# Asking for the small first load, lam, on ScalarE's queue instead of SyncE's

## The chip, the cores and the metric

The kernel runs on one core of a Trainium2 chip. The metric is the device time of one execution in microseconds (us); lower is better. The time quoted for a kernel is the median of its timed runs. A profile is one execution recorded by the hardware profiler; its span runs from the first to the last instruction of the core.

## The reference

The computation is a decayed linear attention over blocks, followed by a gated causal convolution and two projections, all in float32 at 4 batches, 8 heads, 768 positions and 64 channels to a head (the three `moe_` matrices are float64 on the host):

```python
Dmask   = where(i >= j, lam[h] ** (i - j), 0)            # per head, in a block of 64
lam_pow = lam[h] ** (i + 1);  rev_pow = lam[h] ** (63 - i)
for each block of 64 positions:
    intra = ((q k^T) * Dmask) v
    inter = (q * lam_pow) kv_state
    out   = intra + inter
    kv_state = lam[h] ** 64 * kv_state + (k * rev_pow)^T v
x    = out with the heads side by side                   # 4 x 768 x 512
gate = sigmoid(causal convolution of x, 5 taps, per channel, conv_w)
result = (gate * (x @ w_val)) @ w_out
```

`lam` holds eight numbers, one decay to a head. Everything else is built from them and from the four large inputs.

## The kernel before

The kernel works in 12 steps, each of 128 positions of two batches. For each step it loads two tiles of 1 MiB: `lq` (q and k, transposed, line 354, piece `ld.i.0` of the order) and `lv` (v and k by token, line 354, piece `ld.i.2`). The weights come in four loads of 1 MiB, `w_raw` (line 373): two for `w_val` (`wv.0`, `wv.1`) and two for `w_out` (`wo.0`, `wo.1`). A load of 20 KB brings `conv_w` (line 454). Results go out in pieces of 128 or 256 KB.

The order of all work after the opening is written out by hand in the string `ORDER`: each engine runs its instructions in that order, and the framework adds the semaphores. All transfers are requested by SyncE (`SP`) in the order of the string, so a request that has to wait holds up those behind it. The string begins

```
ld.0.0:lq0 dm.0 dm.1 qe ld.0.2:lv0 kd.0.0 s.0.0:s0,s1 kd.0.1 m.0.0.0:A0 s.0.1:u1,u2 m.0.1.0 ia.0.0:xp0 wv.0:g0
ld.1.0:lq1 ld.1.2:lv1 wv.1:g1 m.0.0.1:A1 m.0.1.1 ia.0.1 f.0:u3 wv.0.0.e:val0 ld.2.0:lq2 ...
```

Ahead of the string stands an opening that is not in it. Its first transfer is `lam`, repeated on the host for the 128 partitions (128 x 8 floats, 4 KB, line 191). Then come the identity (GpSimd, `masks.py`), a tile of zeros (VectorE, line 196), a first sigmoid on ScalarE that brings its table load to the front (line 199), and nine warming matmuls on TensorE (line 205; the trace counts them as 18).

Two pieces read `lam`. `dm.0` and `dm.1` (line 233) make the decay mask `mask_c` by eight scans on VectorE, one to a head. `qe` (lines 243 and 246) makes the powers `qdec_c` by repeated doubling on GpSimd. The first reader of the mask is `m.0.0.0` (line 565), which multiplies the first scores (`s.0.0`, TensorE, line 542, from `lq`) by it; it stands behind all eight scans on VectorE. The result `A` goes with `lv` into `ia.0.0` (line 607). The widening of the weights (`wv.0.0.e` and the pieces after it, lines 278 to 320) begins on VectorE when the first `w_raw` has landed; TensorE first needs its product in `v.0.0` (line 946).

On ScalarE nothing of the string comes before the widening of the first weight (line 290).

Of the kernel before, what the change touches and what calls it, by code (L numbers as in the profile page):

```python
# [140 lines left out]
def decay_attention_then_gated_conv(  # L141
# [9 lines left out]
    nc = tc.nc  # L151
# [36 lines left out]


    lam_bc = const.tile([P, H], F32, name="lam_bc")  # L190
    nc.sync.dma_start(lam_bc, lam)
    sdec = const.tile([P, H, D], F32, name="sdec")
    ident = sdec.rearrange("p h d -> p (h d)")[:, :P]
    make_identity(nc, ident)
# [1022 lines left out]
```

## Time and profile before

| | |
|---|---|
| median of 3 runs | 203.88 us |
| runs | 203.19 to 203.99 us |
| profiled execution | 203.55 us |
| its span | 201.6 us |
| mean granted TensorE clock | 1.000 |
| TensorE matmul, busy share of the span | 96% |
| VectorE, busy share | 90% |
| ScalarE, busy share | 65% |
| GpSimd, busy share | 70% |
| `lam` load, request to landing | 1.6 us |

The profile names engines PE (TensorE matmul), PEld (TensorE weight load), DVE (VectorE), ACT (ScalarE), POOL (GpSimd) and SP (SyncE); a `q` behind a name means the engine's sequencer, which issues transfers and waits. `out<-in` are the program's tiles. Times within a trace are microseconds from the start of the span.

### The profile page before, as it was taken

What the parts mean: (1) busy time and instruction counts of PE and PEld (TensorE: products, weight loads), DVE (VectorE), ACT (ScalarE), POOL (GpSimd) and SP (SyncE); (2) the same over time, 40 slices, a digit from 0 to 9 for tenths busy, and PEclk for the clock granted to TensorE, in tenths of its full rate; (3) what the DMA queues carried; (4) which work ended last, traced back from release to release, by engine and by line L of the source; (5) the groups of instructions that cost most, each with busy time, mean ns of one, the idle gap of its engine ahead of it and who ended that gap; (6) DMA issues with size and microseconds to landing.
All of it is one profiled execution on the core that took longest, in us unless ns stands there. A gap on an engine that the chain in (4) does not pass through costs nothing.

```text
span 201.6 us, 7521 instructions
## 1 busy us (share of the span) xinstructions
PE 193.8 (96%) x3282; PEld 166.6 (83%) x3282; DVE 180.9 (90%) x285; ACT 132.1 (65%) x262; POOL 141.8 (70%) x128
## 2 busy tenths in 40 slices
PE   7689999999999999999999999999999999999993
PEld 7568999999899997899888878788777878788882
DVE  5778999998869988998997999999999989999990
ACT  2069589697975698757266455997379953457812
POOL 5447457897799299928946999999959997653000
PEclk9999999999999999999999999999999999999999
DMA  5999999990609103970595992000002210000245
GB/s 180 419 431 423 418 429 419 424 395 26 215 18 367 42 3 83 345 307 3 197 306 187 333 351 99 3 3 7 0 3 104 107 49 3 0 0 2 104 163 202
DMA packets 7952, 36.15 MB, mean 179 GB/s; under 512 B 1136, under 2 KB 1392, under 8 KB 4336
## 3 DMA queue, kind: packets, MB, share of 16 engines
q1 hardware_dynamic: 7920, 35.68, 46.1%
q8 instruction: 25, 0.41, 0.8%
q14 instruction: 7, 0.06, 0.1%
HBM read 29.38 MB, written 6.29 MB: 177 GB/s over the span
## 4 chain that ended last, share of the span: by engine, by line
PE 73%; DVE 9%; DMA 9%; ACT 4%; SPq 2%; issue 1%; ACTq 0%; DVEq 0%
PE vp L946 20%; PE op L1151 18%; PE seven_X L888 11%; DMA lq<-in_qkv 9%; PE xp L592 4%; PE xp L629 4%; PE s L552 4%; PE st L654 4%; PE seven_yz L888 3%; DVE acc L793 3%; PE seven_Z L888 1%; ACT s_part L840 1%; DVE w_sum L405 1%; DVE w_sum L412 1%; SPq L354 1%
## 5 line engine op out<-in xcount | busy, mean ns | idle before, releaser
L793 DVE SCALAR_TENSOR_TENSOR acc<-x,conv_sb,acc 128x512 f32<-128x512 f32 x96 | 70.2, 750 | 5.0 <-ACT acc L791 3.6
L946 PE MATMUL vp<-x_hi,wv_hi 128*128 128x256 f32 (+1 forms) x112 | 34.8, 311 | 0.0
L946 PE MATMUL vp<-x_hi,wv_lo 128*128 128x256 f32 (+1 forms) x112 | 33.5, 299 | 0.3 <-POOL wv_lo L320 0.3
L946 PE MATMUL vp<-x_lo,wv_hi 128*128 128x256 f32 (+1 forms) x112 | 33.4, 298 | 0.0
L1151 PE MATMUL op<-wo_hi,hs 128*128 128x512 f32 x96 | 30.5, 399 | 0.0
L1033 POOL TENSOR_TENSOR hs<-g,hs 128x512 fp32r<-128x512 f32 x12 | 15.9, 1333 | 13.9 <-ACT hs L1022 9.0
L761 POOL TENSOR_TENSOR x_lo<-x,x_hi 128x512 fp32r<-128x512 f32 x18 | 22.9, 1290 | 2.2 <-ACT x_hi L750 2.2
L506 POOL TENSOR_TENSOR qd<-lq,qdec_c 128x512 f32<-128x512 f32 (+1 forms) x18 | 23.1, 1297 | 0.0
L946 PEld LDWEIGHTS vp<-x_hi,wv_hi 128*128 128x128 f32 x112 | 21.3, 190 | 1.6
L946 PEld LDWEIGHTS vp<-x_hi,wv_lo 128*128 128x128 f32 x112 | 21.4, 191 | 1.2 <-POOL wv_lo L320 0.5
L946 PEld LDWEIGHTS vp<-x_lo,wv_hi 128*128 128x128 f32 x112 | 21.4, 191 | 0.6
L791 ACT ACTIVATE acc<-x,conv_sb 128x512 f32<-128x512 f32 x24 | 16.8, 698 | 7.7 <-DVE state L663 7.5
L666 POOL TENSOR_TENSOR sdec<-state,qdec_c 128x512 f32<-128x512 f32 x17 | 20.5, 1207 | 1.0 <-DVE state L663 0.9
L1151 PEld LDWEIGHTS op<-wo_hi,hs 128*128 128x128 f32 x96 | 17.6, 188 | 4.0
L1151 PE MATMUL op<-wo_lo,hs 128*128 128x512 f32 x48 | 18.9, 393 | 0.0
L798 ACT ACTIVATE g<-acc 128x512 f32<-128x512 f32 x24 | 14.0, 597 | 5.7 <-DVE acc L793 5.6
L716 ACT COPY x<-xp 128x512 f32<-128x512 f32 x24 | 12.9, 593 | 3.7 <-PE xp L592 3.2
L1158 ACT COPY o<-op 128x512 f32<-128x512 f32 x16 | 9.4, 587 | 8.0 <-PE op L1151 6.3
L663 DVE TENSOR_TENSOR state<-st,sdec 128x512 f32<-128x512 f32 x17 | 11.7, 686 | 2.0 <-POOL x L723 0.7
L290 ACT ACTIVATE w_em<-w_em,rebias 128x512 int32<-128x512 int32 (+1 forms) x9 | 6.0, 683 | 11.3 <-DVE w_em L278 11.3
L487 ACT ACTIVATE lv<-lv,dmask 128x128 f32<-128x128 f32 x40 | 12.3, 394 | 0.6 <-DMA lv<-in_qkv 0.6
L592 PE MATMUL xp<-A,lv 64*64 64x64 f32 x576 | 12.3, 221 | 0.0
(197 smaller groups left out, 493.4 us busy)
## 6 DMA issues: line engine op xcount, KB each, us to landing
lq<-in_qkv SPq DMA_DIRECT2D x12, 1024.0 KB, 8.0
lv<-in_qkv SPq DMA_DIRECT2D x12, 1024.0 KB, 7.6
out<-o SPq DMA_DIRECT2D x17, 256.0 KB, 3.1
w_raw<-in_w_val SPq DMA_DIRECT2D x2, 1024.0 KB, 12.4
w_raw<-in_w_out SPq DMA_DIRECT2D x2, 1024.0 KB, 17.3
out<-kept SPq DMA_DIRECT2D x6, 256.0 KB, 2.5
out<-o SPq DMA_DIRECT2D x2, 128.0 KB, 2.2
conv_raw<-in_conv_w SPq DMA_DIRECT2D x1, 20.0 KB, 15.8
```

What stands on the lines that cost most here:

```text
L506: nc.gpsimd.tensor_tensor(out=s["qd"][:, hs, ms], in0=lds[i]["qT"][:, u].rearrange("p h (m i) -> p h m i", m=2)[:, :, ms], in1=qdec[:, hs, ...
L592: nc.tensor.matmul(s["xp"][rows(hh), b ^ m, b, g, :], lds[i]["v"][rows(m), b, h * D : (h + 1) * D], s["A"][rows(m), b, h, :], start=b == 0 ...
L666: nc.gpsimd.tensor_tensor(out=sdec, in0=state, in1=qdec_c[:, :, n - 1 : n].to_broadcast([P, H, D]), op=ALU.mult)
L716: nc.scalar.copy(*blocks(s["x"], b))
L761: nc.gpsimd.tensor_tensor(out=s["x_lo"][:, ts], in0=s["x"][:, ts], in1=s["x_hi"][:, ts].bitcast(F32), op=ALU.subtract)
L791: nc.scalar.mul(to, src, w)
L793: nc.vector.scalar_tensor_tensor(out=to, in0=src, scalar=w, in1=to, op0=ALU.mult, op1=ALU.add)
L798: nc.scalar.activation(xu[un]["g"][:, ct].rearrange("p u (b i) -> p b u i", b=NB2), xu[un]["acc", ct].rearrange("p b (u i) -> p b u i", u= ...
L888: nc.tensor.matmul(s[n, f][:, cut], ww[:, t, fs], xx[:, t, cut], start=k in (1, 2, 5) and m == 0, stop=k in (2, 3, 4) and m == 3 * HU - 1, ...
L946: nc.tensor.matmul(to, w[:, ct, fs], xx[:, ct], start=n_mm == 0, stop=n_mm == 3 * NT - 1)
L1033: (either() if halves else nc.vector if direct else nc.gpsimd).tensor_tensor(out=to, in0=x["h", j, fs], in1=x["to", j, fs].bitcast(F32), o ...
L1151: nc.tensor.matmul(s["op", b, j][:, cols], hh, w[:, ft, cols], start=ft == 0 and n == 0, stop=ft == NT - 1 and n == 2,)
```

## The change

The request for `lam` is issued by ScalarE's queue. SyncE's first request is then the first `lq`. Nothing else is changed: the string `ORDER`, the tiles and the shapes are as they were.

```diff
@@ -188,7 +188,7 @@
     lam_bc = const.tile([P, H], F32, name="lam_bc")
-    nc.sync.dma_start(lam_bc, lam)
+    nc.scalar.dma_start(lam_bc, lam)
     sdec = const.tile([P, H, D], F32, name="sdec")
     ident = sdec.rearrange("p h d -> p (h d)")[:, :P]
     make_identity(nc, ident)
```

## Rows read from the trace of the kernel before

**Rows 1.** The page, parts 1 and 4: busy shares, and the chain by engine.

```profile
PE 193.8 (96%) x3282; PEld 166.6 (83%) x3282; DVE 180.9 (90%) x285; ACT 132.1 (65%) x262; POOL 141.8 (70%) x128
...
PE 73%; DVE 9%; DMA 9%; ACT 4%; SPq 2%; issue 1%; ACTq 0%; DVEq 0%
```

**Rows 2.** The chain that ended last, in order: start, length, what.

```profile
0.74 0.38 SPq L191
...
4.52 17.59 DMA lq<-in_qkv
...
22.16 2.06 PE s L542 x32
...
113.94 1.00 PE s L552 x64
...
114.96 0.68 DVE state L663
...
198.47 0.37 ACT o L1119
```

**Rows 3.** Timeline from 0 to 14 us: start, length, instruction, [idle before it <-releaser].

```profile
0.73 1.28 ACT L199 ACT_TABLE_LOAD   x1 [0.73 <-PEq L1198]
...
0.74 0.38 SPq L191 DMA_DIRECT2D lam_bc<-in_lam  x1
...
1.05 4.21 PE L205 MATMUL warm<-zero 128*128 128x128 f32 x18 [1.05 <-DVE zero L196]
1.17 0.42 SPq L354 DMA_DIRECT2D lq<-in_qkv  x1
...
2.02 0.20 ACT L199 ACTIVATE preload<-zero 128x1 f32<-128x1 f32 x1
...
2.38 0.20 POOL L243 COPY qdec_c<-lam_bc 128x8 f32<-128x8 f32 x1 [1.08 <-DMA lam_bc<-in_lam]
2.43 4.02 DVE L233 TENSOR_TENSOR_SCAN mask_c<-lam_bc,sdec 128x128 f32<-128x128 f32 x8 [1.42 <-DMA lam_bc<-in_lam]
...
6.48 2.06 PE L542 MATMUL s<-lq 64*128 64x128 f32 x32 [1.22 <-DMA lq<-in_qkv]
7.67 2.48 DVE L565 TENSOR_TENSOR A<-s,mask_c 128x512 f32<-128x512 f32 x4 [1.22 <-PE s L542]
...
9.01 2.09 PE L607 MATMUL xp<-A,lv 128*64 128x128 f32 x32 [0.47 <-DVE A L565]
...
11.35 0.43 DVE L278 TENSOR_SCALAR w_em<-w_raw 128x512 int32<-128x512 int32 x1 [1.19 <-DMA w_raw<-in_w_val]
...
11.81 0.72 ACT L290 ACTIVATE w_em<-w_em,rebias 128x512 int32<-128x512 int32 x1 [9.58 <-DVE w_em L278]
```

**Rows 4.** Stretches of 0.1 us; the last columns are TensorE's clock, DMA share, GB/s.

```profile
1.70:1.80 0.10, 0.10 (x2) 0.10 (x2) 0.00 (x0) 0.10 (x1) 0.00 (x0) 1.00 0.18 12
1.80:1.90 0.10, 0.10 (x3) 0.10 (x2) 0.00 (x0) 0.10 (x1) 0.00 (x0) 1.00 0.39 21
1.90:2.00 0.10, 0.10 (x2) 0.10 (x2) 0.00 (x0) 0.10 (x1) 0.00 (x0) 1.00 0.15 8
...
2.10:2.20 0.10, 0.10 (x2) 0.10 (x2) 0.00 (x0) 0.10 (x1) 0.00 (x0) 1.00 0.00 0
2.20:2.30 0.10, 0.10 (x3) 0.10 (x2) 0.00 (x0) 0.03 (x1) 0.00 (x0) 1.00 2.30 492
```

**Rows 5.** Stretches of 2 us, same columns.

```profile
2.00:4.00 2.00, 2.00 (x12) 2.00 (x11) 1.57 (x5) 0.22 (x2) 1.22 (x6) 1.00 0.85 242
...
20.00:22.00 2.00, 2.00 (x64) 1.80 (x64) 1.97 (x5) 0.44 (x1) 0.00 (x0) 1.00 1.00 422
```

**Rows 6.** Timeline from 6 to 30 us, TensorE's two waits behind 12 us.

```profile
13.85 2.06 PE L542 MATMUL s<-lq 64*128 64x128 f32 x32 [0.62 <-DMA lq<-in_qkv]
...
16.65 0.39 PE L946 MATMUL vp<-x_hi,wv_lo 128*128 128x256 f32 x1 [0.32 <-POOL wv_lo L320]
```

**Rows 7.** Waits of SyncE's queue: us in total, times, longest.

```profile
SPq L373 <- DMA w_raw<-in_w_val: 1.4, 1, 1.4
```

## The prediction

> **What bounds the kernel now.** I read the page first, for what is full: TensorE is busy 96% of the span and carries 73% of the chain that ended last [rows 1]. Then the chain in order of time. Its head is not TensorE: it begins with SyncE's request for `lam`, goes through SyncE's next requests and then through 17.59 us of a load of `lq`. At 22.16 it passes to TensorE, which it leaves for the first time at 114.96, for VectorE [rows 2]. So for 22 us the loads set the pace, and after that the engines do, one behind the other, with no gap of size down to the last eviction at 198.47.
>
> Third, the opening instruction by instruction. `lam` is requested at 0.74; the request holds SyncE for 0.38 us, and the first `lq` is requested at 1.17, 0.43 us after `lam` [rows 3]. TensorE's warming ends at 1.05 + 4.21 = 5.26, and it then waits 1.22 us for that `lq`, until 6.48. VectorE waits 1.19 us for the first `w_raw`, until 11.35 [rows 3], and TensorE 0.62 us for the second `lq`, until 13.85 [rows 6]. Each of these waits ends with a landing. From 6.48 to 13.85 three loads land, 2.46 us apiece, and 1 MiB at the 422 GB/s of a full stretch [rows 5] takes 2.48 us. The stream is a full pipe: each landing is its start plus what stands ahead of it.
>
> Fourth, how the pipe starts. `lam`'s packets run from 1.70 to 2.00, 0.97 us behind their request. Then the transfer engines stand still, and the heavy packets begin in the stretch 2.20 to 2.30 [rows 4], 1.03 us behind the first `lq`'s request, a like delay. So the pipe does not wait for `lam`'s bytes to be out of the way; it waits for its own request, which waits for SyncE to be through with `lam`'s.
>
> **The change, part by part.**
>
> Removed from SyncE: one request, worth 1.17 - 0.74 = 0.43 us [rows 3]. Every later request of SyncE that waits for nothing moves up by that, and the heavy packets would begin near 1.79. `lam`'s packets load the engines for (0.18 + 0.39 + 0.15) x 0.1 = 0.07 us on the mean [rows 4], whichever queue sends them; before and after contain them once. The gain at the pipe's start is thus 0.43 us at most, and 0 at least, if the two queues hinder each other fully. I take 0.43, since the engines stand idle in the stretch that the heavy packets would move into.
>
> Added to ScalarE: one request. No row shows one on that queue; the nearest is SyncE's own, 0.38 us. On ScalarE it stands ahead of the table load (0.73, 1.28 us) and the first sigmoid (2.02, 0.20 us) [rows 3], both of which it pushes back, and the next instruction there, at 11.81, is preceded by 9.58 us idle. Above it is bounded by that cover, below by nothing; I take 0 on the path. Without the cover it would cost 0.4 us.
>
> Moved: the landing of `lam`. Its readers are the powers on GpSimd (2.38) and the scans on VectorE (2.43 to 6.45), behind which the first use of the mask stands, at 7.67, after 1.22 us of waiting for scores [rows 3]. With the scores 0.43 us earlier, `lam` still has 1.22 - 0.43 = 0.79 us of room before any reader notices. Past that point there is more: TensorE has 0.62 us in front of the second `lq`'s scores and 0.32 us in front of the first projection that needs the low half of the weight [rows 6], and these two gaps are ended by landings (the second by the chain that begins with `w_raw` at 11.35). So `lam` costs nothing at the end until it is 0.79 + 0.94 = 1.73 us late, and the gain is used up at 2.16 us.
>
> Waits among SyncE's requests: the twelfth, for `w_out`, goes to a buffer not used before and still waited 1.4 us for the landing of the first `w_val` load, which is the fourth [rows 7]. So a request waits for the one eight places ahead. With `lam` gone from the list both lose one place and the pairs stay as they are; only the ninth, whose partner was `lam`, loses its partner. Cost 0.
>
> What is downstream moves with the stream. The engines' waits up to 16.65 end with landings or with work that a landing began, and every wait behind them is on another engine or on a buffer that is given back, so all move by the same 0.43 us. What does not move is the warming (5.26), the scans (6.45) and the powers, and each of these ends before its reader would start.
>
> Sum: -0.43 us. On the profiled execution that is 203.55 - 0.43 = 203.12 (span 201.6 - 0.43 = 201.17, and 1.95 us around it as before). The median of the runs shown is 0.33 us above the profiled execution, so the prediction for a median is 203.88 - 0.43 = 203.45 us, -0.2%. A measurement of this kernel can tell about 0.5%, 1.0 us, from no change, since its own runs lie 0.8 us apart; the forecast is below that.
>
> **The rivals.**
>
> *The two requests hinder each other at the source.* If the first `lq`'s packets start where they did, because its request is served behind `lam`'s though another queue sends it, the gain is 0: 203.88. For it: only one queue is in use in the trace, so no row shows two side by side. Against it: the 0.43 us were SyncE's own time, and it is ScalarE that spends them now. [...]
>
> *`lam` takes turns with the load.* Its 128 pieces, one to a partition, are eight to each of 16 engines, as a 1 MiB load's 128 rows of 8 KB are; an engine then needs 2.48 / 8 = 0.31 us for a row. If each piece of `lam` has to let one row go first, its last is out at 1.79 + 8 x 0.31 = 4.27, and read 0.38 us later (2.00 to 2.38 before [rows 3, 4]), at 4.65. The mask is ready at 4.65 + 0.05 + 4.02 = 8.72, against 7.24 for the scores; 1.48 us late, of which 0.94 are absorbed and 0.43 paid by the gain: +0.11, 204.0 us. Against it: `lam`'s packets took 0.30 us in all [rows 4] and would be nearly out before the first rows come. [...]
>
> *The other side: slower.* If the table load goes first on ScalarE, `lam` is requested at 2.01 instead of 0.74, and without turns is read at 2.01 + 1.64 = 3.65, 0.48 us too late for 7.24, which is absorbed. With eight turns on top, 2.48 us, it is read at 6.13; the mask is ready at 10.20, 2.96 us late; less 0.94 and 0.43 that is +1.59, 205.5 us. It decides from a `lam` read later than 2.38 + 2.16 = 4.54. For it: the load's row starts at 0.73, the engine's first moment. Against it: it takes both halves, and the row of the sigmoid, 2.02, follows the load at once [rows 3], as it would if the load belonged to that instruction. [...]
>
> *More than the request.* From 2.22 to 4.00 the pipe is not full: 242 GB/s over 2.00 to 4.00 [rows 5] are 484 KB, 1.14 us' worth at 422, so 0.64 us are lost. If that ramp is also shorter when the loads come first, the gain is up to 1.07: 202.8 us. Nothing in the rows says why it would be.
>
> **How the numbers follow.** The forecast, 203.45, gets 0.55; no gain through the source 0.17; turns, 0.13; both halves of the slower rival 0.06; the ramp as well 0.09. Faster by over 0.5% (below 202.86): half of the ramp's case, and some 0.07 of the forecast's, by scatter of the runs; together 0.12. Slower by over 0.5% (above 204.90): the slower rival and 0.01 of the turns; 0.07. The rest, 0.81, is the same. The range: low is the lowest run of before, 203.19, less 0.43 and half of the ramp's 0.64, 202.4. High is the highest run, 203.99, and the slower rival with half its turns: `lam` read at 4.89, 1.72 us late for the scores, +0.35 at the end, with 0.1 to round; 204.5. That leaves out the rest of the slower rival and of the ramp's case and some scatter, under 2 in 10.
>
> **What would show it.** In the profile after: `lam`'s request on ACT near 0.73, ahead of the table load; the first `lq` near 0.74; heavy packets near 1.8; `lam` read before 3.2; TensorE's first scores near 6.05, the first `w_raw` at 10.92, the second `lq`'s scores at 13.42, and the third's at 21.7 instead of 22.16; the whole chain behind, shifted by the same 0.43. Wrong would be: heavy packets still at 2.2 (source), scans that end behind the first scores (turns), a table load ahead of the request (slower), a shift that is there at 22 us and gone at 115 (something that I did not see holds a fixed time), or more than 1.95 us around the span for a second queue.

## The result, and the profile after

The changed kernel takes 206.57 us (median of 6 runs, 205.65 to 207.27), the kernel before, on the same chip, 203.91 (6 runs, 203.19 to 205.00). The ratio is 1.0124 [1.0083, 1.0165]: slower by 1.2%. On another chip, 205.96 against 204.05, it was 1.0098 [1.0063, 1.0134]. The forecast was 203.45 us, in 202.4 to 204.5. Medians here and in the table below are of all runs, while the ratios leave out single runs that fell into a slower state of the chip.

The profiled execution took 205.65 us with a span of 203.8, so 1.85 us lie around the span, against 1.95 before. All of the loss is inside it. The page of the changed kernel, parts 1, 3 and 4 (busy shares; queues with packets, MB and share of the transfer engines' time; the chain by engine):

```profile
PE 195.1 (96%) x3282; PEld 167.8 (82%) x3282; DVE 181.8 (89%) x285; ACT 132.0 (65%) x262; POOL 142.3 (70%) x128
...
q10 hardware_dynamic: 144, 0.00, 0.0%
...
PE 72%; DVE 14%; ACT 6%; DMA 4%; issue 2%; ACTq 0%; DVEq 0%
```

Beside [rows 1] the work is the same, and a queue q10 is new: ScalarE's, with 144 packets, which is `lam`'s 128 pieces of 32 bytes and 16 packets of 4 bytes. The chain in order of time (start, length, what), beside [rows 2]:

```profile
0.73 5.39 DMA lam_bc<-in_lam
6.22 1.43 DVE mask_c L233 x5
...
11.48 2.99 PE xp L607 x28
...
200.61 0.37 ACT o L1119
```

Its head is no longer the stream of loads. It is the landing of `lam`, which took 5.39 us instead of 1.6, and behind it VectorE's scans. The timeline of the changed kernel, 0 to 26 us (start, length, instruction, [idle before it <-releaser]), beside [rows 3, 6]:

```profile
0.73 0.40 ACTq L191 DMA_DIRECT2D lam_bc<-in_lam  x1
0.74 0.37 SPq L354 DMA_DIRECT2D lq<-in_qkv  x1
1.17 1.28 ACT L199 ACT_TABLE_LOAD   x1 [1.17 <-PEq L1198]
...
5.95 2.06 PE L542 MATMUL s<-lq 64*128 64x128 f32 x32 [0.77 <-DMA lq<-in_qkv]
6.17 0.20 POOL L243 COPY qdec_c<-lam_bc 128x8 f32<-128x8 f32 x1 [4.87 <-DMA lam_bc<-in_lam]
6.22 4.03 DVE L233 TENSOR_TENSOR_SCAN mask_c<-lam_bc,sdec 128x128 f32<-128x128 f32 x8 [5.21 <-DMA lam_bc<-in_lam]
10.17 2.45 DVE L565 TENSOR_TENSOR A<-s,mask_c 128x512 f32<-128x512 f32 x4
...
12.55 0.41 DVE L278 TENSOR_SCALAR w_em<-w_raw 128x512 int32<-128x512 int32 x1
13.41 1.35 POOL L499 TENSOR_TENSOR qd<-lq,qdec_c 128x512 f32<-128x512 f32 x1 [1.00 <-DMA lq<-in_qkv]
13.75 1.56 DVE L298 SCALAR_TENSOR_TENSOR w_em<-w_raw,w_em 128x512 int32<-128x512 int32 x1
16.93 2.06 PE L542 MATMUL s<-lq 64*128 64x128 f32 x32
17.37 1.27 POOL L320 TENSOR_TENSOR wv_lo<-w_em,wv_hi 128x512 fp32r<-128x512 f32 x1 [2.61 <-ACT wv_hi L316]
24.55 2.06 PE L542 MATMUL s<-lq 64*128 64x128 f32 x32
```

The gain is there: the first `lq` is requested at 0.74 and the first scores begin at 5.95 instead of 6.48. But the scans begin at 6.22 instead of 2.43 and end at 10.25, 2.24 us behind the end of those scores (8.01). `A` follows 2.50 us later than before (10.17 against 7.67). Behind `A` on VectorE stands the widening of the first weight, 12.55 against 11.35: VectorE's wait of 1.19 us for `w_raw` [rows 3] is gone, which absorbs about half of the lateness. From there to the third scores the delay grows again, to 24.55 - 22.16 = 2.39, and it is 2.14 at the last eviction (200.61 against 198.47).

Why `lam` lands late is seen in the DMA queues of the changed kernel, here in the stretches 2.5 to 3, 4.5 to 5 and 5.5 to 6 us (q1 is SyncE's, q10 ScalarE's; packets, MB, share of the engines' time):

```profile
q1 hardware_dynamic: 19, 0.16, 98.8%
q10 hardware_dynamic: 18, 0.00, 1.9%
...
q1 hardware_dynamic: 32, 0.21, 105.2%
q10 hardware_dynamic: 31, 0.00, 3.5%
...
q1 hardware_dynamic: 29, 0.22, 104.5%
q10 hardware_dynamic: 4, 0.00, 0.5%
```

Over 2.5 to 5.0 us both queues sent 119 packets: one small piece, one row of 8 KB, in turn. In the trace's records of single packets, 126 of `lam`'s 128 pieces are followed within 0.01 us by a packet of SyncE's queue. The pieces use 2 to 4% of the engines' time, but each waits for a row. Spread evenly over the 16 engines of the page, which is an estimate, 144 packets are nine to an engine, and 119/16 = 7.4 turns in 2.5 us are 0.34 us each. The first `lq` has as many rows as `lam` has pieces, 128 each, so when the two alternate they end together: `lq` is used from 5.95 on, `lam` from 6.17.

What adds to the delay behind 12 us is twofold. First, VectorE's second step of the widening (line 298) takes 1.56 us, beginning at 13.75 while GpSimd's `qd` (13.41 to 14.76) runs. In the kernel before it began ahead of `qd` and took 0.69:

```profile
12.56 0.69 DVE L298 SCALAR_TENSOR_TENSOR w_em<-w_raw,w_em 128x512 int32<-128x512 int32 x1
```

Second, TensorE has no work from 8.01 to 10.88, and after that the clock falls, as the windows of the changed kernel show (stretch, its length, busy us and instructions of PE, PEld, DVE, ACT and POOL, granted clock, DMA share, GB/s):

```profile
9.00:10.00 1.00, 0.00 (x0) 0.00 (x0) 1.00 (x2) 0.00 (x0) 0.97 (x1) 1.00 1.01 426
...
12.00:13.00 1.00, 1.00 (x14) 1.00 (x12) 1.00 (x4) 0.01 (x1) 0.41 (x1) 0.50 1.05 442
```

The granted clock is 0.50 from 11.8 to 15.2 us; the 28 products that begin at 11.48 take 2.99 us, where 32 took 2.09 before [rows 3], and the second scores begin 3.08 us late (16.93 against 13.85).

### The profile page after: what moved, and what is told of

It is laid out like the page before. It is cut to its first block, busy times and chain, and to the rows that moved or that the text cites. A ratio compares the mean times of both kernels' runs of the same rounds, so it can differ in the third digit from the quotient of the medians.

```text
span 203.8 us, 7521 instructions
## 1 busy us (share of the span) xinstructions
PE 195.1 (96%) x3282; PEld 167.8 (82%) x3282; DVE 181.8 (89%) x285; ACT 132.0 (65%) x262; POOL 142.3 (70%) x128
## 4 chain that ended last, share of the span: by engine, by line
PE 72%; DVE 14%; ACT 6%; DMA 4%; issue 2%; ACTq 0%; DVEq 0%
PE vp L946 21%; PE op L1151 12%; PE seven_X L888 10%; DVE acc L793 5%; PE xp L592 4%; PE xp L629 4%; PE s L552 4%; PE st L654 3%; PE seven_yz L888 3%; PE xp L607 3%; DMA lam_bc<-in_lam 3%; PE s L542 2%; DVE mask_c L233 2%; DMA out<-o 2%; PE st L646 2%
## 5 line engine op out<-in xcount | busy, mean ns | idle before, releaser
L320 POOL TENSOR_TENSOR wv_lo<-w_em,wv_hi 128x512 fp32r<-128x512 f32 x4 | 5.3, 1319 | 10.4 <-ACT wv_hi L316 10.4
```

## The experiments

Theory: `lam`'s pieces wait for rows of the load, the mask comes late, and VectorE's order makes that the time. Rivals: ScalarE's queue is slow in itself; a second queue costs something else, with the lateness of `lam` harmless; the price is not the lateness but the clock, or the collision of VectorE with GpSimd. Ratios are against the kernel before on the same chip.

| kernel | us (runs) | before | ratio | `lam` read | third scores |
|---|---|---|---|---|---|
| before, profiled | 203.91 (6) | | | 2.38 | 22.16 |
| after | 206.57 (6) | 203.91 | 1.0124 [1.0083, 1.0165] | 6.17 | 24.55 |
| after, again | 205.96 (7) | 204.05 | 1.0098 [1.0063, 1.0134] | 6.11 | 24.35 |
| e1_twin | 204.79 (10) | 204.28 | 1.0031 [0.9998, 1.0064] | 2.62 | 22.59 |
| e2_mirror | 205.69 (4) | 204.28 | 1.0104 [1.0041, 1.0167] | 2.52 | 22.89 |
| e3_behind | 206.32 (10) | 204.28 | 1.0091 [1.0060, 1.0122] | 6.17 | 23.22 |
| e4_one_row | 204.05 (10) | 204.28 | 1.0001 [0.9976, 1.0026] | 3.91 | 21.56 |
| e5_fills | 206.02 (6) | 204.05 | 1.0102 [1.0067, 1.0136] | 6.36 | 24.32 |
| e6_rows_4k | 204.96 (11) | 204.05 | 1.0044 [1.0016, 1.0072] | 5.33 | 23.95 |
| e7_rows_2k | 206.11 (10) | 204.05 | 1.0091 [1.0061, 1.0121] | 3.90 | 23.07 |
| e9_fills_qd_later | 205.83 (7) | 204.04 | 1.0077 [1.0040, 1.0114] | 5.99 | 23.06 |
| e10_qd_later | 205.93 (6) | 204.04 | 1.0099 [1.0064, 1.0134] | 6.11 | 24.49 |

**e1_twin.** The change, with a second copy of `lam` asked for on SyncE ahead of `lq`. Nothing reads the copy; it only puts `lq` back to where its request was.

```diff
     nc.scalar.dma_start(lam_bc, lam)
+    twin = const.tile([P, H], F32, name="twin")
+    nc.sync.dma_start(twin, lam)
```

> Lam stays on ScalarE's queue; SyncE asks for a second copy of lam (into a spare tile) ahead of the first lq, so that the loads' rows start 0.43 us later than in the changed kernel. Turns (lam's pieces alternate with the loads' 8 KB rows): the two small transfers are out by 2.1, before the first row; lam is read at 2.4 to 2.7 and the time is that of before, 203.9 +- 0.4. The queue itself (a first request on ScalarE's queue takes some 5 us to land, whatever else runs): lam is still read near 6.2, and the time is 206.5 to 207.

The timeline of e1_twin, 0 to 10 us:

```profile
2.67 4.02 DVE L235 TENSOR_TENSOR_SCAN mask_c<-lam_bc,sdec 128x128 f32<-128x128 f32 x8 [1.67 <-DMA lam_bc<-in_lam]
...
6.39 3.72 PE L544 MATMUL s<-lq 64*128 64x128 f32 x32 [1.12 <-DMA lq<-in_qkv]
```

On the same queue of ScalarE, `lam` is read at 2.62 when no load runs beside it. The queue is not slow, and most of the loss is gone. The time, 204.79, is 0.5 us above that of before on this chip, a little more than the 0.4 allowed for; the profiled execution lost 1.1 us near 172 us, at a place described in the last section. In this execution the first scores took 3.72 us instead of 2.06, with the same matmuls. One of them took 418 ns at the median, against 272 in the changed kernel. That the clock was still low there is an estimate, from e2, where the same products took up to 419 ns in a stretch that reads 0.50; the windows of e1 read 1.00 from 1 to 10 us. As e3 shows the same (3.79 us, 418 ns), it is not put down to this edit.

**e2_mirror.** The kernel before, with the first `lq` on ScalarE's queue and all else on SyncE's.

```diff
-                nc.sync.dma_start(t, src[:, lo : lo + 2])
+                (nc.scalar if (i, lo) == (0, 0) else nc.sync).dma_start(t, src[:, lo : lo + 2])
```

> The kernel before with the two requests exchanged: lam on SyncE's queue, the first lq on ScalarE's. Turns: lam alternates with the rows of lq, no matter which of the two queues it is on; it is read between 5.3 and 6.3, and the time is 205.5 to 206.8. The queue itself: lam is read at 2.4 as before, the first lq lands late or as before, and the scans do not wait; 203.5 to 204.5.

The timeline of e2_mirror, 0 to 11 us:

```profile
1.03 0.41 ACTq L354 DMA_DIRECT2D lq<-in_qkv  x1
...
7.64 2.93 PE L542 MATMUL s<-lq 64*128 64x128 f32 x32 [2.38 <-DMA lq<-in_qkv]
```

Neither expectation came out. ScalarE's request began only at 1.03, 0.29 us behind `lam`'s, and `lam` was read at 2.52. But `lq` was then asked for only 0.14 us ahead of `lv` (1.03, 1.17), and the first scores came at 7.64 instead of 6.48. The engines had moved 2.0 MB by 7.5 us (the GB/s of the windows from 1 to 7.5 us, added up), nearly the 2.1 MB of both loads. By that estimate `lq` shared the engines with `lv`, the same sharing between other partners. What it costs is not settled by four runs between 204.36 and 207.43, and it tells nothing of `lam`.

**e3_behind.** One queue, SyncE's, with `lam` behind the first `lq`: the lateness without the second queue.

```diff
-    nc.sync.dma_start(lam_bc, lam)
...
                 nc.sync.dma_start(t, src[:, lo : lo + 2])
+                if (i, lo) == (0, 0):
+                    nc.sync.dma_start(lam_bc, lam)
```

> One queue only: SyncE asks for the first lq, then for lam, then for lv. Lam is read behind the first lq, at 5.0 to 6.3. If lam's lateness alone is the price, the time is 205.5 to 206.8, as in the changed kernel. If the second queue costs something else beside, it is under 204.6.

The timeline of e3_behind, 0 to 26 us:

```profile
6.22 4.02 DVE L232 TENSOR_TENSOR_SCAN mask_c<-lam_bc,sdec 128x128 f32<-128x128 f32 x8 [5.21 <-DMA lam_bc<-in_lam]
...
13.74 0.69 DVE L297 SCALAR_TENSOR_TENSOR w_em<-w_raw,w_em 128x512 int32<-128x512 int32 x1
13.84 1.74 POOL L500 TENSOR_TENSOR qd<-lq,qdec_c 128x512 f32<-128x512 f32 x1 [1.44 <-DMA lq<-in_qkv]
...
23.22 2.06 PE L543 MATMUL s<-lq 64*128 64x128 f32 x32
```

The scans begin at 6.22, to the hundredth as in the changed kernel, and the time is 1.0091 of before, inside the intervals of the changed kernel's two comparisons. So the lateness is enough for the loss; a second queue has no price of its own that these intervals show. The turns made `lam` exactly as late as if it had been put behind the whole first load. In this execution VectorE's step came 0.1 us ahead of GpSimd's `qd` and took 0.69, and as its first scores took 3.79 us, TensorE's wait behind them was only 1.11 us and the clock did not fall (1.00 in all windows from 6 to 18 us). The third scores are 1.33 us earlier than in the changed kernel. The profiled execution is the lowest of its ten runs (204.68), so its timeline is not that of the median.

**e4_one_row.** `lam` as one row of 32 bytes on ScalarE's queue, one piece in place of 128; a TensorE product with a row of ones, put among the warming matmuls, spreads it over the partitions. The row lies in spare room of `state`.

```diff
+    lam_row, ones = flat[0:1, 256 : 256 + H], flat[0:1, :P]
+    nc.scalar.dma_start(lam_row, lam[0:1])
+    spread = psum.tile([P, H], F32, name="spread", tag="u3", bufs=1)
...
+        if n == 4:
+            nc.tensor.matmul(spread, ones, lam_row, start=True, stop=True)
+    nc.vector.tensor_copy(lam_bc, spread)
```

> Lam stays on ScalarE's queue, but only one row of 32 B is loaded; TensorE spreads it over the partitions by a product with ones, between the warming matmuls, and VectorE copies it out. Turns: one piece needs one turn, it is there by 2.9, the scans start by 3.4 and end by 7.5, and the 0.43 us of the earlier loads are kept: 203.2 to 203.8. The queue itself: the row is there near 6, and the time is 206.3 or more.

The timeline of e4_one_row, 0 to 24 us:

```profile
3.96 4.03 DVE L240 TENSOR_TENSOR_SCAN mask_c<-lam_bc,sdec 128x128 f32<-128x128 f32 x8
7.91 2.45 DVE L572 TENSOR_TENSOR A<-s,mask_c 128x512 f32<-128x512 f32 x4
10.80 0.43 DVE L285 TENSOR_SCALAR w_em<-w_raw 128x512 int32<-128x512 int32 x1 [0.44 <-DMA w_raw<-in_w_val]
...
21.56 2.06 PE L549 MATMUL s<-lq 64*128 64x128 f32 x32
```

With the pieces gone the loss is gone, second queue and all. The scans are 1.53 us late and cost nothing, which is the room that the prediction worked out, and the stream's gain arrives: `w_raw` 0.55 us earlier, the third scores 0.60. The last eviction is 1.43 earlier (197.04), but that is not all the stream's: 0.4 of it comes between 37 and 76 us, where each of the other profiles gains as much on the one of the kernel before. The scans start 0.6 us later than expected, since TensorE came to the spreading product only at 3.05. The timed runs do not show a gain: 1.0001, give or take 0.25%, and the profiled execution (202.85) is the lowest of its ten. So this is the predicted change, made to work, and its gain is too small for the timed runs, as the forecast said of its own. It is not a version that was shown to beat the kernel before.

**e6_rows_4k and e7_rows_2k.** The change, with the first `lq` asked for in two requests of 4 KB rows, or four of 2 KB rows (the diff is that of the first). By the theory of turns a piece then waits a half or a quarter as long.

```diff
-                nc.sync.dma_start(t, src[:, lo : lo + 2])
+                if (i, lo) == (0, 0):
+                    for a in range(2):
+                        nc.sync.dma_start(t[:, a], src[:, a])
+                else:
+                    nc.sync.dma_start(t, src[:, lo : lo + 2])
```

> The changed kernel with the first lq asked for in two requests whose rows are 4 KB instead of 8 KB; the same bytes. Turns: lam waits for as many rows as before, each half as long; it is read at 4.0 to 4.8 instead of 6.2, and the time is 0 to 0.5 us above that of before. If lam waits for something else than rows (a fixed delay of its queue, or a whole load), it is read at 6 or behind.

> The same in four requests with rows of 2 KB: lam is read at 3.2 to 3.9, which is inside the room that it has, and the 0.4 to 0.5 us of the earlier loads are kept: 0.996 to 0.999 of the kernel before. Without turns: as the changed kernel.

The timeline of e6_rows_4k, the reading of `lam`:

```profile
5.33 0.20 POOL L243 COPY qdec_c<-lam_bc 128x8 f32<-128x8 f32 x1 [4.03 <-DMA lam_bc<-in_lam]
```

Its DMA queues, 4 to 4.5 us (columns as above):

```profile
q1 hardware_dynamic: 54, 0.17, 90.7%
q10 hardware_dynamic: 52, 0.00, 5.6%
```

Still one to one, and about twice as many of each as with 8 KB rows in that half microsecond (25 and 26). `lam` is read at 5.33 and, with 2 KB rows, at 3.90, the latter as expected, the former 0.5 us later than expected. The order of the three, 6.17, 5.33, 3.90, is that of the row's size. The time follows at 4 KB, 1.0044, though by 0.9 us above that of before, where at most 0.5 was expected. At 2 KB, where 0.996 to 0.999 was expected, it is 1.0091. The timeline of e7_rows_2k, 0 to 26 us, shows a part of why:

```profile
0.74 1.80 SPq L356 DMA_DIRECT2D lq<-in_qkv  x4
...
3.90 0.20 POOL L243 COPY qdec_c<-lam_bc 128x8 f32<-128x8 f32 x1 [2.60 <-DMA lam_bc<-in_lam]
...
12.37 0.43 DVE L278 TENSOR_SCALAR w_em<-w_raw 128x512 int32<-128x512 int32 x1 [2.03 <-DMA w_raw<-in_w_val]
```

Its mask is in time, but now the loads are late: four requests hold SyncE for 1.80 us, the transfers move 268 to 352 GB/s from 4 to 7 us, and `w_raw` is in hand at 12.37 instead of 11.35. In the profile that makes the third scores 0.91 us late and the last eviction 0.68 (199.15), about a third of the changed kernel's delay (2.39 and 2.14). The rest of the timed 1.9 us does not come from this; in the profiled execution 1.05 us of it lie behind the last eviction.

**e5_fills, e10_qd_later, e9_fills_qd_later.** The change, with the two things that grow behind 12 us taken away one at a time and then together: two more groups of fills in TensorE's idle stretch, so that the clock stays up (`FILL = 3`, `f.0:u3 f.1:u0` ahead of `ia.0.0`, `f.2:u3` at the old place), and GpSimd's `qd.1.1` moved in the string so that VectorE's step does not meet it.

```diff
-FILL = 1
+FILL = 3
...
-... m.0.1.0 ia.0.0:xp0 wv.0:g0
+... m.0.1.0 f.0:u3 f.1:u0 ia.0.0:xp0 wv.0:g0
...
-... xl.0 st.0:u1 qd.1.1:qd0
+... xl.0 st.0:u1
...
-... m.1.0.0 dc wv.0.0.l v.0.0:u0 m.1.0.1:A1 x.0:x0 qd.1.0
+... m.1.0.0 dc wv.0.0.l v.0.0:u0 m.1.0.1:A1 x.0:x0 qd.1.1:qd0 qd.1.0
```

> The changed kernel with two more filling matmuls of TensorE (2.2 us of work on zeros, nothing reads it) between the first scores and the first product that needs the mask, where TensorE stood idle for 2.9 us. If the fall of the granted clock to 0.5 that follows this idle stretch is a part of the price, the clock stays at 1.0, the second lq's scores start near 15.6 instead of 16.93, and the time falls by 0.8 to 1.5 us against the changed kernel. If VectorE's late mask is the whole price, the time is that of the changed kernel within 0.3 us.

> The changed kernel with only GpSimd's product moved. The step on VectorE takes 0.69, but TensorE, at half its clock, starts the second lq's scores near 16.8 as in the changed kernel, and the projection behind them near 18.8: 0 to 0.4 us under the changed kernel, 1.007 to 1.011. If the collision alone is the second part of the price: 0.8 us or more under it.

> The changed kernel with the two fills of the fills experiment, and with GpSimd's first product of q (qd.1.1) moved behind the first low half of the weight, so that it does not run beside VectorE's first bitwise step on the weight (which took 1.56 us in the changed kernel, 0.69 before). Collision and clock each hide the other: with both gone, the step takes 0.69 again, the low half of the weight starts near 16.6 instead of 17.4, the first projection passes at 17.8, and the time is 0.7 to 1.2 us under the changed kernel, 1.004 to 1.007 of the kernel before. If the late mask reaches the end in another way: 1.009 to 1.011, as with the fills alone.

The timeline of e5_fills, 12 to 26 us:

```profile
13.94 1.58 DVE L298 SCALAR_TENSOR_TENSOR w_em<-w_raw,w_em 128x512 int32<-128x512 int32 x1
15.81 2.06 PE L542 MATMUL s<-lq 64*128 64x128 f32 x32
17.58 1.28 POOL L320 TENSOR_TENSOR wv_lo<-w_em,wv_hi 128x512 fp32r<-128x512 f32 x1 [2.61 <-ACT wv_hi L316]
```

The timeline of e10_qd_later, the same stretch:

```profile
13.68 0.69 DVE L298 SCALAR_TENSOR_TENSOR w_em<-w_raw,w_em 128x512 int32<-128x512 int32 x1
16.55 1.28 POOL L320 TENSOR_TENSOR wv_lo<-w_em,wv_hi 128x512 fp32r<-128x512 f32 x1 [4.22 <-ACT wv_hi L316]
16.86 2.06 PE L542 MATMUL s<-lq 64*128 64x128 f32 x32
```

With the clock up (1.00 in all windows from 5 to 20 us), TensorE is early (15.81) and then waits for `wv_lo`, which the collision holds to 17.58. Without the collision `wv_lo` is early (16.55) and TensorE is late (16.86), its 28 products behind the wait having taken 2.82 us against 2.07 in e5, which is put down to the low clock. Each hides the other, and neither alone moves the third scores (24.32, 24.49). The timeline of e9_fills_qd_later, with both gone:

```profile
15.43 2.06 PE L542 MATMUL s<-lq 64*128 64x128 f32 x32
16.32 1.28 POOL L320 TENSOR_TENSOR wv_lo<-w_em,wv_hi 128x512 fp32r<-128x512 f32 x1 [4.11 <-ACT wv_hi L316]
23.06 2.06 PE L542 MATMUL s<-lq 64*128 64x128 f32 x32
```

The third scores are 1.49 us earlier than in the changed kernel, as expected. The timed gain is not settled: 1.0077 [1.0040, 1.0114], where 1.004 to 1.007 was expected, overlaps both of the changed kernel's intervals, and e10 on the same chip takes 205.93 against e9's 205.83, though its third scores are 1.43 us later. In e9's profile the delay against the kernel before goes from 0.98 us to 2.09 near 172 us (last section), so in that execution most of the gain at the head is lost again there. The 0.90 us that stay at the third scores (23.06 against 22.16) are what the lateness leaves without the two.

## Why the prediction was wrong

**What held.** The request on ScalarE stands ahead of the table load (0.73, 1.17) and costs nothing there: the next work on that engine, at 12.99, stands behind 10.33 us idle. SyncE's 0.43 us went: the first rows move in the stretch 1.70 to 1.80, and the first scores are 0.53 us earlier, of which 0.43 were forecast. The rivals "hinder each other at the source" and "table load first" are thereby out, and so is a price around the span (1.85 against 1.95). The two requests do hinder each other, but the loss falls on `lam`'s: asked for at 0.73, its pieces begin behind 2.1, 1.4 us later, where it took 0.97 before. The room was right as far as it was tried: 1.53 us late cost nothing in e4, where the bound was 1.73.

**The step that failed** is the weight given to turns, 0.13, and the sentence it rests on: that `lam`'s packets took 0.30 us in all and would be nearly out before the first rows come. That was read from a trace in which `lam` had the engines to itself for half a microsecond, and the change takes away just that half microsecond. After it both requests start together, the rows come first (1.70 to 1.80; `lam`'s first pieces are out after 2.0), and each piece waits for a row. `lam` was read at 6.17, where the forecast wanted it before 3.2 and the slower rival's point was 4.54.

**The rival was mis-sized as well.** It put the reading at 4.65, from eight turns of 0.31 us that begin at 1.79. By the count of packets there were nine (144 over 16 engines, evenly spread); they took 0.34 us while both queues ran; and the pieces began after 2.0. From 2.1 on that ends at 5.2, and read 0.4 later at 5.6. The plainer slip is that 0.31 us is a row's time in a full stretch, which the load's start is not: the prediction itself read 242 GB/s there [rows 5], and it put the first scores, which begin when these very rows have landed, at 6.05. One row to a piece means that `lam` lands with the load, so near 6.05, and 6.17 was measured. The slower rival's size, read at 6.13 and 205.5 us, was nearly met, but by luck: the turns alone did it, with no table load ahead. e1 (no load beside it), e4 (one piece) and the order of e6 and e7 (smaller rows) each take the turns away or shorten them, and `lam` comes earlier each time.

**From lateness to time.** With the real reading put into the prediction's own working, the mask is ready at 10.25, 3.01 us after the shifted scores would have ended their wait (7.24); less 0.94 and 0.43 that is +1.64, 205.5 us. The runs show +2.66 and +1.91, and e3, on one queue, +2.04. So this step carries most of the loss, though by another path than it was put: the room was not only in TensorE's two gaps, it was VectorE's 1.19 us in front of `w_raw`, because `A` and the widening stand in one order on VectorE behind the scans. Without collision and clock that leaves +0.90 at the third scores (e9) and +1.06 (e3). Collision and low clock, which the late `lam` brings about here, make it +2.39.

**What stays open.** Executions of one kernel differ by about a microsecond by things that a profile of one of them need not show. Three are seen in the profiles: how long the first scores take (2.06 or 3.7 us); a race on VectorE and GpSimd near 172 us, below; and the last stores, with which the span ends 3.1 to 3.3 us behind the last eviction in seven profiles (3.17 before) and 3.8 to 4.2 in five (the second one of the changed kernel, e4, e5, e7, e9). So a median can lie a microsecond from what its profile explains: in e3 the last eviction is 0.84 us late, the median 2.04. How much of the timed loss beyond +0.90 belongs to the collision, to the clock and to a changed chance of such a race was not settled. The recorded spans of the single runs bear on it: among executions of one kernel, those whose mean granted clock is 0.995 or more are the shorter, on the mean by 1.05 us in the second set of the changed kernel (two against five), 0.74 in e3 (five against four) and 1.15 in e6 (four against seven). In the first set of the changed kernel all six lie at 0.988 to 0.992, and the loss is the largest, +2.66. But e5, whose runs all keep the clock, is no faster. Whether e4's gain exists in the timed runs is open below 0.25%.

## What to carry to other kernels

A second queue saved the requesting engine's time here (0.43 us), but the transfer engines served the two queues in turn, packet by packet (119 to 119 over 2.5 us). A small transfer cut into many pieces then waited one big row per piece (0.34 us), so count it as rows and not as its bytes: with as many pieces as the load beside it had rows, 128 each, it landed when that load did (here 4 KB, used at 6.17, with 1 MiB, used at 5.95). Keep such a transfer on the same queue ahead of the bulk (`lam` read at 2.38), or make it one piece (3.91 in e4, with the spreading). When a measured transfer was alone in the trace, its duration says nothing of the same transfer beside another one; and before calling it harmless, follow its reader's engine in order to the next thing queued behind it.

## What the runs showed of the hardware that was not expected

VectorE and GpSimd can hold each other up. The step of line 298 takes 0.69 us alone and 1.56 when GpSimd's product began 0.34 us earlier; VectorE's step beginning first, it is GpSimd's product that is longer (1.74 in e3 against 1.28 in the kernel before). VectorE's step ends 0.55 us behind the end of GpSimd's product (15.31 and 14.76), nearly a whole step of its own. By what means the one holds up the other was not shown. The step of line 310 is not held up: in e6 it began at 14.23, inside GpSimd's product (13.80 to 15.07), and took 0.69 us as elsewhere. One of its inputs lies in PSUM by the kernel; whether that makes the difference was not tried.

The same race comes again late in the kernel. The timeline of e9_fills_qd_later, 170 to 175 us:

```profile
172.10 1.29 POOL L1033 TENSOR_TENSOR h_lo<-g,h_hi 128x512 fp32r<-128x512 f32 x1 [1.18 <-ACT h_hi L1022]
172.15 1.79 DVE L412 TENSOR_TENSOR w_sum<-w_sum 128x512 f32<-128x512 f32 x1
```

And of the kernel before, the same stretch:

```profile
171.13 1.87 POOL L1033 TENSOR_TENSOR h_lo<-g,h_hi 128x512 fp32r<-128x512 f32 x1 [1.21 <-ACT h_hi L1022]
171.17 0.67 DVE L412 TENSOR_TENSOR w_sum<-w_sum 128x512 f32<-128x512 f32 x1
```

GpSimd is recorded 0.04 or 0.05 us ahead both times, yet in one VectorE pays 1.1 us and in the other GpSimd pays 0.6. The profiles of e1, e9 and the second one of the changed kernel have the former, and across it their delay against the kernel before grows by 1.1 us. The recorded starts do not tell which of the two pays; a small shift from the head of the kernel may be worth 1.1 us there, which was not tried by itself.

TensorE's clock fell to 0.50 after one idle stretch of 2.87 us (8.01 to 10.88), and read 0.50 from 11.8 to 15.2 although TensorE worked throughout, while the same opening in e5 and e9, with the gap filled, kept 1.00 (in the windows from 5 to 20 and from 11 to 16 us). In e2 it fell after a wait of 2.38 us (0.62 on the mean from 8.5 to 9 us, 0.50 from 9 to 12); in the kernel before, waits of 1.22 and 0.47 us left it at 1.00.
